# A four-layer attention and ReLU network on one core: reciprocals of two chunks spread by one set of DMAs, add and ReLU fused on VectorE, queues in a new order

## The chip, the cores and the metric

The kernel runs on one core of a Trainium2 chip. The metric is the time of one execution on the device, in microseconds (us); the median of several runs is compared. In the profile PE is TensorE (matmuls) and PEld its weight loads, DVE is VectorE, ACT is ScalarE, POOL is GpSimd, and SP is SyncE, which here only issues DMAs. "L960" is line 960 of the kernel before.

## What is computed

Four layers, each added to the residual x of 2048 tokens by 512: linear attention with 32 heads of 16, a feed-forward block with ReLU, and the same two again with the same weights.

```python
def _A_ref(x, wqkv, wo):
    qkv = (x @ wqkv).reshape(B, S, 3, H, Dh).transpose(2, 0, 3, 1, 4)   # H = 32, Dh = 16
    q, k, v = qkv[0], qkv[1], qkv[2]
    phi = lambda t: jnp.where(t > 0, t + 1, jnp.exp(t)) + 1e-6
    pq, pk = phi(q), phi(k)
    kv = jnp.einsum("bhsd,bhse->bhde", pk, v)
    z = jnp.einsum("bhsd->bhd", pk)
    num = jnp.einsum("bhqd,bhde->bhqe", pq, kv)
    den = jnp.einsum("bhqd,bhd->bhq", pq, z)[..., None] + 1e-6
    return (num / den).transpose(0, 2, 1, 3).reshape(B, S, D) @ wo

def _B_ref(x, w1, w2):                      # Dff = 1376
    return jnp.maximum(x @ w1, 0) @ w2

x = x + _A_ref(_layernorm(x), A_wqkv, A_wo)
x = x + _B_ref(_layernorm(x), B_w1, B_w2)
x = x + _A_ref(_layernorm(x), A_wqkv, A_wo)
x = x + _B_ref(_layernorm(x), B_w1, B_w2)
```

## The kernel before

**Tiling.** The 2048 tokens are 16 tiles of 128 (on the partitions), and four chunks of four tiles. The residual `xres` stays on chip in float32, the normalized input `xn` and its transpose `Tb` in float16. Layers 0 and 2 are attention, layers 1 and 3 the feed-forward block. Steps of a layer start as soon as the chunks that they need are there, so the end of one layer and the start of the next share the engines.

**Attention** goes in this order. For each chunk the keys and queries are projected (L980, L1193; some chunks by a seven-product scheme, L1032, whose last step on DVE is an `em` and a `phi`), and the sums over all tokens that give G are built up as chunks arrive (`g0_m_t`, `g1_m_t`, L1132; the 0 and 1 are the two halves of the keys, m a block of the input, t a chunk). In the steps `pq` and `bar` (L1758, L1780) the row of G for the normalization is evicted (`gevz`), gives z (`zcol`, `zc`), and with it the denominators: `den t` (L1216) multiplies the queries of chunk t by z on PE, with a block of 32 columns of the array per head group; ACT takes the logarithm (`lnd`, L1222) and the exponential of its negative (`rdc`, L1224), which is the reciprocal. One reciprocal belongs to 16 rows of the queries (the 16 positions of a head), and a tile of `rdc` has each of them four times; so a DMA spreads each block of 32 rows over 128 partitions (`spread t_j`, L1230, four DMAs of 128 KB per chunk, issued by SP). DVE multiplies the queries with the spread reciprocals, two blocks j at a time (`pqs t_0`, `pqs t_2`, L1237, line 1242 in the profile). Beside that PE combines G with the value weights (`kv`, L1158; for it DVE has subtracted a row from them in four parts, `wvless0` to `wvless3`, L1115), DVE masks the result (`kvmask0`, `kvmask1`, L1165), PE multiplies it by wo (`m0` to `m3`) and it is evicted as Mf (`mev`). Last, in the step `p2` (L1804), `fin i_0` and `fin i_2` (L1245) multiply the queries of tile i by Mf, four matmuls of 128x512 per tile (ps<-Mf,big in the profile, 64 of them), and `resid i` (L964) adds the residual. Then come the statistics of the next normalization (ACT squares, POOL and DVE the small ones, `rstd`, `nbias`), the normalization itself (`norm i`, L886), and the transposing DMA (`tr t_k`, L902) that the next layer's first matmul needs.

**The feed-forward block** computes x @ w1 in a seven-product scheme over 2x2 blocks (`b_h7`, L1396). Of its four quarters two leave PSUM by a plain ReLU (`hc11`, `hc21`, L1428) and two by an addition (`hc12`, `hc22`, L1437): a partial product in PSUM plus another that ACT saved in SBUF. The sum is written without ReLU, and when the second of the two is there, one more instruction applies ReLU to the whole row of both, in place (`hc22r`):

```python
def add(name, cs, bank, other, okeys, second, half, first):
    ...
    g.add(DVE, lambda e: e.tensor_tensor(ap, sh(psv[:, bank, 0:w]), sh(other()), ALU.add), ...
    if half == 0:
        first_half[0] = qk
        return
    ...
    g.add_flex([(ACT, lambda e: e.activation(row, row, ACTF.Relu), ...),
                (DVE, lambda e: e.tensor_scalar(row, row, 0.0, None, ALU.max), ...)], ...
```

The second product (`b_out`, L1563) has seven products per chunk too, after sums on DVE (`ssum`, L1530).

**What sets the order.** Each operation is entered in program order with the keys that it reads and writes, and gets a priority: its place in that order plus a hint from the table `HINTS` (L63, L445), by its name with the layer in front. Each engine's queue, SP's too, is sorted by priority, and each engine takes the first of its queue alone (`WINDOW` is 1 everywhere, L60), so an instruction that waits holds up all behind it on its engine. An operation with several engines to choose from (`add_flex`, L454) takes the one that a hint ending in "!" names. The durations in the file serve a planner (`_list_schedule`, L465) that gives out PSUM banks and fixes the waits.

Of the kernel before, what the change touches and what calls it, by code (L numbers as in the profile page):

```python
# [6 lines left out]

# [55 lines left out]
HINTS = {"0.aqsum1": -44, "0.aqsum1!": 0, "0.aqsum2": -5, "0.aqsum2!": 0, "0.aqsum3": -114, "0.aqsum3!": 0, "0.aqsum4": 0,  # L63
# [546 lines left out]
def build_kernel(nc, A_x, A_wqkv, A_wo, B_w1, B_w2, out, n_layers_pairs=2, K_STT=0, Q_STT=0, windows=None,  # L610
# [20 lines left out]
    with es:  # L631
# [11 lines left out]
        GT = sb("GT", [128, 4, 512], BF16)  # L643
        KVT = sb("KVT", [128, 4, 128], BF16)
        Mf = sb("Mf", [128, 4, 512], BF16)
        NL = 2
        FIN_SPLIT = 4
        SPLIT_H = 4
        SPLIT_TREV = 1
# [106 lines left out]
        def unit_ap(u, p=128):  # L756
            return big[0:p, u * 512:(u + 1) * 512]
# [638 lines left out]
        def b_h7(t, tw):  # L1396
# [40 lines left out]
            def add(name, cs, bank, other, okeys, second, half, first):  # L1437
# [3 lines left out]
                def sh(x):  # L1441
                    return x.rearrange("p (a k) -> p a k", k=256)
# [539 lines left out]
```

## Time and profile before

| | us |
|---|---|
| median of 3 runs | 261.85 (261.5 to 262.0) |
| profiled execution, first to last instruction (span) | 260.5 |
| PE busy | 255.2 (98%) |
| DVE busy | 230.8 (89%) |
| ACT busy | 206.3 (79%) |
| POOL busy | 60.0 (23%) |

The profiled execution's time is given as its span; what lies around the span is not recorded. Busy times are unions of the intervals in which an engine has an instruction in work. A matmul is drawn to the modelled end of its pipeline, so two that follow each other at full rate overlap. Some matmul records are missing (125 of 128 matmuls with Mf are there), which leaves short gaps that are none. In a row of the timeline "x16" says that 16 instructions of one kind are merged, and the bracket at its end how long the engine stood idle before it, and what ended that. A row of the table by stretches gives for each engine busy time and count, then the granted clock of PE, the share of the DMA engines and GB/s.

### The profile page before, as it was taken

How to read it: one execution, taken by the hardware profiler on the slowest of the kernel's cores; microseconds unless marked ns; L12 is line 12 of the kernel's file. 1: busy time of each engine (PE TensorE's matmuls, PEld its weight loads, DVE VectorE, ACT ScalarE, POOL GpSimd, SP SyncE). 2: the span in 40 equal slices, each digit the busy share in tenths (PEclk: the TensorE clock that was granted, in tenths of full speed). 3: DMA queues.
4: the chain of work that ended last, by engine and by line, in shares of the span. 5: the costliest groups of instructions: out<-in, count | busy, mean ns of one | idle time of the engine just before them, and what ended most of it. 6: DMA issues, size and time to landing. Idle time of an engine off the chain costs nothing.

```text
span 260.5 us, 5876 instructions
## 1 busy us (share of the span) xinstructions
PE 255.2 (98%) x2165; PEld 198.3 (76%) x2176; DVE 230.8 (89%) x572; ACT 206.3 (79%) x446; POOL 60.0 (23%) x163
## 2 busy tenths in 40 slices
PE   7999999999999999999999999999999999999995
PEld 3554577744788988889888878674388989888884
DVE  5999997799999999999989999858999998876684
ACT  4999999689999969999998899766899928853100
POOL 4100000037844015341420430003777000000000
PEclk9999999999999999999999999999999999999999
DMA  6767950754343062222130040057251414300104
GB/s 195 288 161 140 324 183 18 178 122 94 65 89 64 17 86 44 40 42 43 31 72 0 4 81 1 3 136 174 59 102 38 83 23 126 58 20 3 81 3 161
DMA packets 46268, 22.46 MB, mean 86 GB/s; under 512 B 35904, under 2 KB 44704, under 8 KB 46240
## 3 DMA queue, kind: packets, MB, share of 16 engines
q1 hardware_dynamic: 45968, 21.83, 34.8%
q10 hardware_dynamic: 272, 0.26, 0.4%
q8 instruction: 17, 0.28, 0.4%
q14 instruction: 11, 0.09, 0.1%
HBM read 7.14 MB, written 2.10 MB: 35 GB/s over the span
## 4 chain that ended last, share of the span: by engine, by line
PE 82%; DVE 5%; DMA 4%; SPq 4%; ACT 3%; issue 1%; DVEq 0%
PE ps L960 81%; SPq L1234 4%; DMA big<-rdc 3%; DVE xres L967 3%; DVE big L1242 1%; ACT lnd L1222 1%; DMA xin<-in_A_x_dram 1%; PE ps L919 1%; ACT rdc L1224 1%; DVE bst L851 0%; ACT big L1073 0%; DVE xin L1391 0%; PE ps L846 0%; ACT escr L1090 0%; ACT GT L1144 0%
## 5 line engine op out<-in xcount | busy, mean ns | idle before, releaser
L975 ACT ACTIVATE sqscr<-xres 128x512 bf16<-128x512 f32 x48 | 29.7, 621 | 4.4 <-DVE xres L967 3.0
L960 PE MATMUL ps<-w,big 128*128 128x256 bf16 (+1 forms) x256 | 32.6, 272 | 0.0
L960 PE MATMUL ps<-big,xn 128*128 128x256 bf16 (+1 forms) x221 | 31.6, 287 | 0.3
L702 ACT ACTIVATE ps<-ps 128x512 f32<-128x512 f32 (+1 forms) x41 | 22.7, 563 | 11.1 <-PE ps L960 11.1
L960 PE MATMUL ps<-Mf,big 128*128 128x512 bf16 x125 | 28.8, 379 | 0.7 <-DVE big L1242 0.5
L960 PEld LDWEIGHTS ps<-w,big 128*128 128x128 bf16 (+1 forms) x256 | 24.9, 98 | 3.1
L960 PEld LDWEIGHTS ps<-big,xn 128*128 128x128 f16 x224 | 21.5, 98 | 6.1 <-issue 0.7
L1443 DVE TENSOR_TENSOR big<-ps,escr 128x512 bf16<-128x512 f32 (+1 forms) x38 | 22.7, 600 | 3.6 <-PE ps L960 2.3
L960 PEld LDWEIGHTS ps<-Mf,big 128*128 128x128 bf16 x128 | 12.0, 98 | 15.8 <-DVE big L1242 2.0
L960 PE MATMUL ps<-Tb,w 128*128 128x256 f16 x160 | 23.7, 273 | 0.0
L960 PE MATMUL ps<-xn,xin 128*128 128x256 f16 x160 | 23.2, 273 | 0.0
L960 PE MATMUL ps<-xn,w 128*128 128x256 f16 x160 | 22.4, 273 | 0.0
L873 POOL TENSOR_SCALAR mean<-s 128x2 f32<-128x2 f32 x24 | 8.4, 350 | 56.0 <-DVE xres L967 53.5
L899 ACT ACTIVATE xn<-xres,nbias,rstd 128x512 f16<-128x512 f32 x26 | 20.7, 816 | 0.7 <-POOL nbias L883 0.6
L1462 ACT ACTIVATE escr<-ps 128x512 f32<-128x512 f32 (+1 forms) x38 | 19.2, 536 | 2.4 <-PE ps L960 2.3
L1431 ACT ACTIVATE big<-ps 128x512 bf16<-128x512 f32 (+1 forms) x38 | 19.0, 533 | 1.9 <-PE ps L960 1.8
L960 PE MATMUL ps<-wqkv,Tb 128*128 128x512 bf16 (+1 forms) x93 | 19.7, 342 | 0.1
L881 POOL TENSOR_TENSOR rstd<-veps,nhalf 128x2 f32<-128x2 f32 x24 | 18.4, 768 | 5.1 <-DVE veps L879 4.5
L960 PEld LDWEIGHTS ps<-Tb,w 128*128 128x128 bf16 x160 | 15.5, 98 | 2.5 <-DVE w L1391 0.4
L960 PE MATMUL ps<-w,Tb 128*128 128x96 bf16 (+2 forms) x176 | 17.3, 224 | 0.0
L960 PEld LDWEIGHTS ps<-xn,w 128*128 128x128 bf16 x160 | 15.4, 98 | 2.0
L960 PEld LDWEIGHTS ps<-xn,xin 128*128 128x128 bf16 x160 | 15.2, 98 | 2.0 <-DVE xres L967 0.2
(146 smaller groups left out, 626.1 us busy)
## 6 DMA issues: line engine op xcount, KB each, us to landing
big<-rdc SPq DMA_DIRECT2D x32, 128.0 KB, 2.7
w<-in_B_w_dram SPq DMA_DIRECT2D x1, 1376.0 KB, 7.2
w<-in_B_w_dram SPq DMA_DIRECT2D x1, 1280.0 KB, 10.4
xin<-in_A_x_dram SPq DMA_DIRECT2D x2, 512.0 KB, 6.5
wqkv<-in_A_wqkv_dram SPq DMA_DIRECT2D x3, 256.0 KB, 4.9
xin<-in_A_x_dram SPq DMA_DIRECT2D x4, 128.0 KB, 3.1
xin<-in_A_x_dram SPq DMA_DIRECT2D x2, 256.0 KB, 4.9
wqkv<-in_A_wqkv_dram SPq DMA_DIRECT2D x1, 512.0 KB, 4.1
```

Of the source, the lines that this page charges most:

```text
L702: g.add(ACT, lambda e: e.activation(psv[:, b, 0:w], psv[:, src, 0:w], ACTF.Identity), [("ps", src)], [("ps", b)], C_ACT_PSUM if w == 512 e ...
L873: g.add(POOL, lambda e: e.tensor_scalar(mean[:, sl], s1[:, sl], -INV_D, None, ALU.mult), [("s1", i) for i in tl], [("mean", i) for i in tl ...
L881: g.add(POOL, lambda e: e.tensor_tensor(rstd[:, sl], veps[:, sl], nhalf[:, 0:n], ALU.pow), [("veps", lo), ("nhalf",)], [("rstd", i) for i ...
L899: (ACT, lambda e: e.activation(xn[:, i, :], src, ACTF.Identity, scale=rstd[:, i:i + 1], bias=nbias[:, i:i + 1]), C_ACT_SB_AP)],
L919: last = e.transpose(psb()[:, 128 * q:128 * q + 128], xn[:, i, 128 * c:128 * c + 128], ident[:])
L960: last = e.matmul(o, l, r, start=st, stop=sp, skip_group_check=skip)
L967: g.add(DVE, lambda e: e.scalar_tensor_tensor(xres[:, i, :], psv[:, b, :], 0.0, src, ALU.add, ALU.add, accum_out=s1[:, i:i + 1]), [("ps", ...
L975: g.add(ACT, lambda e: e.activation(sqscr[:, q, :], xres[:, i, :], ACTF.Square, scale=math.sqrt(INV_D), accum_out=s2[:, i:i + 1]), xr(i), ...
L1234: dma(lambda e, j=j, u=u: e.dma_start(unit_ap(u), rdc[32 * j:32 * j + 32, t, :].unsqueeze(1).broadcast_to([32, 4, 512])), [("rdc", t)], [( ...
L1431: g.add_flex([(ACT, lambda e: e.activation(ap, src(), ACTF.Relu), C_ACT_PSUM if w == 512 else 270.0), (DVE, lambda e: e.tensor_scalar(ap, ...
L1443: g.add(DVE, lambda e: e.tensor_tensor(ap, sh(psv[:, bank, 0:w]), sh(other()), ALU.add), [("ps", bank)] + okeys + ([] if first else bk), q ...
L1462: g.add(ACT, lambda e, w=w: e.activation(q[:, 0:w], psv[:, bank, 0:w], ACTF.Identity), [("ps", bank)], key, C_ACT_PSUM if len(cs) == 2 els ...
```

## The change

Three parts, and a new table of hints.

*Spreads.* The reciprocals of chunks 0 and 1 are computed first, and each of the four DMAs then spreads both chunks, 256 KB instead of 128. The rows of both chunks lie side by side in source and target, so a DMA has as many descriptors as before, of twice the length. Chunk 2 and chunk 3 stay as they were.

```diff
+        SPREADS = ((0, 1), (2,))
...
-        def a_spread(t, first_layer):
-            late = 500.0 if first_layer and t == 0 else 0.0
+        def a_spread(t, n=1):
             for j in range(4):
                 u = rb_unit(t, j)
-                dma(lambda e, j=j, u=u: e.dma_start(unit_ap(u), rdc[32 * j:32 * j + 32, t, :].unsqueeze(1).broadcast_to([32, 4, 512])),
-                    [("rdc", t)], [("big", u)], 650.0, "spread%d_%d" % (t, j), issue=620.0, late=late)
+                dma(lambda e, j=j, u=u: e.dma_start(big[:, u * 512:(u + n) * 512],
+                                                    rdc[32 * j:32 * j + 32, t:t + n, :].rearrange("p n k -> p (n k)").unsqueeze(1)
+                                                    .broadcast_to([32, 4, 512 * n])),
+                    [("rdc", t + k) for k in range(n)], [("big", u + k) for k in range(n)], 650.0 * n, "spread%d_%d" % (t, j), issue=620.0)
...
-                        for u in range(NCH - 1):
-                            a_den(u)
-                            a_spread(u, first_layer)
+                        for grp in SPREADS:
+                            for u in grp:
+                                a_den(u)
+                            a_spread(grp[0], len(grp))
```

*Add and ReLU.* The additions `hc12` and `hc22` of layers 1 and 3 become one VectorE instruction that adds and clamps the sum to the range from 0 to the largest float32; the row ReLU `hc22r` goes.

```diff
+                if H_SAT:
+                    g.add(DVE, lambda e: e._custom_dve(dve_ops.TENSOR_ADD_SAT, out=ap, in0=sh(psv[:, bank, 0:w]), in1=sh(other()), s0=FMAX, s1=0.0),
+                          [("ps", bank)] + okeys + ([] if first else bk), qk + (bk if first else []),
+                          C_DVE_PSUM if len(cs) == 2 else 335.0, name="%s_%d_%d" % (name, t, cs[0]))
+                    return
```

*More choices.* The first normalization of tiles 6 to 15 and the four `wvless` may run on POOL; by the hints `fnorm8` and `fnorm9` do, `wvless` stays on DVE. Which engine computes the reciprocal root of the first normalization is written as a list, with the same result as before.

```diff
-                g.add_flex([(DVE, f, C_DVE_NORM_BF)],
+                g.add_flex([(DVE, f, C_DVE_NORM_BF)] + ([(POOL, f, C_POOL_NORM)] if i >= PE_TILES else []),
```

*Hints.* Of 1584 hints for places that both tables have, 59 are the same. Of the choices of an engine in layers 1 and 3, 13 of the plain ReLUs (`hc11`, `hc21`) move to DVE and 7 to ACT; the eviction `trev2` of the head, a copy of a transposed tile, moves to DVE. Some hints of layer 0, with the place that they give (place in program order plus hint; lower goes first):

| | before | after |
|---|---|---|
| den0, den1, den2 (PE) | 299, 321, 319 | 291, 298, 301 |
| spread2_2, spread2_3 (SP) | 331, 334 | 314, 310 |
| spread0_0 to spread0_3 (SP) | 324, 320, 314, 310 | 319, 323, 330, 326 |
| pqs2_2, wvless3, kvmask0 (DVE) | 358, 163, 326 | 332, 337, 346 |
| pqs3_0, pqs3_2, resid4, resid6 (DVE) | 432, 435, 416, 428 | 409, 415, 418, 428 |
| last of spread3, load of w2 (L805), tr0_0 (SP) | 407, 199, 434 | 389, 392, 422 |

Sorted by these, and by those of their neighbours, the queues stand as follows around the change (a group `g0_1_2` or `q7_3_4` is four matmuls of 128x256, g0_3_t four of 128x512).

```
layer 0, SP   before  spread0 (x4), spread2 (x4), spread1 (x4), spread3 (x4)      [w2 long before]
              after   spread2_3, spread2_2, spread0 with 1 (x4), spread2_1, spread2_0, spread3 (x4), w2, tr0_0, tr0_1
layer 0, PE   before  q7_2_4 g0_2_1 q7_3_7 den0 g0_0_3 g0_1_3 g0_2_2 g0_2_3 q7_3_4 kv0_0 kv0_1 kv0_2 den2 den1 kv0_3 g1_0_0
              after   q7_2_4 zcol g0_2_1 g0_2_2 den0 g0_1_2 g0_0_3 den1 den2 q7_3_7 g1_2_0 g0_2_3 g0_1_3 g1_0_0 g1_0_1 g1_2_1
                      g1_0_2 kv0_0 g1_0_3 kv0_1 q7_3_4 g1_1_0 kv0_2 g1_1_1 g1_1_2 kv0_3
              before  kv1_1 fin1_0 kv1_2 kv1_3 fin0_0 m2 m3 den3 fin2_0
              after   kv1_1 m1 m0 kv1_2 kv1_3 den3 m3 m2 fin0_0 fin2_0
layer 0, DVE  after   qc7_3_22_add wvless2 pqs2_2 wvless3 qc7_3_21_em qc7_3_21_phi kvmask0 kvmask1 pqs0_0 pqs1_0 pqs0_2 pqs1_2
layer 2, SP   before  spread0_0 0_1 1_1 1_0 0_3 0_2 1_2 1_3 2_3 2_2 2_0 2_1 3_1 3_3 3_2 3_0
              after   spread0 with 1 (x4) spread2_2 2_3 2_1 2_0 3_0 3_2 3_3 3_1
layer 2, PE   before  den0 den1 den2 ... m1 den3
              after   den0 den1 q7_3_7 kv0_0 kv0_1 g1_2_1 g1_0_1 g1_0_2 kv0_2 kv0_3 q7_3_4 g1_0_3 g1_1_0 g1_1_1 g1_1_2 g1_1_3 m0 den2
                      g1_2_2 g1_2_3 m1 kv1_0 kv1_1 den3
layer 2, DVE  before  resid1 resid0 pqs2_2 resid2 resid3 pqs2_0 resid4 resid5 nbias0 resid7 resid6 var4 pqs3_0 veps4 nbias2 pqs3_2
              after   resid1 pqs2_2 resid0 pqs2_0 resid3 var0 resid2 resid4 nbias0 pqs3_2 pqs3_0 resid5
head, PE      before  trp2 qh0_0_0_0 qh0_0_3_0 trp3         after  trp2 qh0_0_0_0 qh0_0_2_0 qh0_0_3_0 trp3 kproj2
```

More of the change, by code (lines that the diff above doesn't have):

```diff
@@ L6 @@
 from concourse import alu_op_type
+from concourse import dve_ops
 ALU = alu_op_type.AluOpType
@@ L646, in build_kernel @@
         NL = 2
+        SPREADS = ((0, 1), (2,))
+        H_SAT = True
+        FMAX = 3.4028234663852886e38
         FIN_SPLIT = 4
@@ L654, in build_kernel @@
         MID_LAST = ()
-        FIRST_ACT_TILES = 4
+        RSTD_ACT = (0, 1, 2, 3, 6, 8, 12)
+        PE_TILES = 6
         lnd = sb("lnd", [128, NL, 512], F32)
@@ L1116, in wv_less_last @@
             for m in range(4):
-                g.add(DVE, lambda e, m=m: e.tensor_tensor(wqkv[:, m, 2 * D:3 * D], wqkv[:, m, 2 * D:3 * D], wvl[:], ALU.subtract),
-                      [("wv0",), ("wvl",)], [("wv", m)], 335.0, name="wvless%d" % m)
+                f = (lambda e, m=m: e.tensor_tensor(wqkv[:, m, 2 * D:3 * D], wqkv[:, m, 2 * D:3 * D], wvl[:], ALU.subtract))
+                g.add_flex([(DVE, f, 335.0), (POOL, f, C_POOL_ADD)], [("wv0",), ("wvl",)], [("wv", m)], name="wvless%d" % m)
         def ones_col(lo, n):
@@ L1676, in ln_first @@
             for i in range(4 * t, 4 * t + 4):
-                if t < FIRST_PE_CHUNKS and i < 6:
+                if i < PE_TILES:
                     ln_stats_first(i, [("xn", i - 2)] if 2 <= i < 4 else [])
@@ L1684, in ln_first @@
             if t == 1:
-                ln_part_first(6, 8)
-                ln_norm(6, True)
-                ln_norm(7, True)
-                tr_dma(1, 1)
+                for i in range(PE_TILES, 8, 2):
+                    ln_part_first(i, i + 2)
+                    ln_norm(i, True)
+                    ln_norm(i + 1, True)
+                    tr_dma(1, i // 2 - 2)
             if t >= FIRST_PE_CHUNKS:
@@ L1815, in p2 @@
                         a_den(NCH - 1)
-                        a_spread(NCH - 1, first_layer)
+                        a_spread(NCH - 1)
                         a_pqs(2)
```

4 lines of the change are left out of this document (2 added, 2 removed), and 519 rows, old and new, of the table HINTS.

## The prediction

> **What bounds the kernel now.** I read the page first (part 1, part 4), then the table by stretches of 5 us, the waits, and the timeline of the two stretches that the table singles out. In order: two lines of the page; five stretches (PE busy, then PE's weight loads, DVE, ACT, POOL, granted clock, DMA share, GB/s); two rows of the waits.
>
> ```profile
> PE 255.2 (98%) x2165; PEld 198.3 (76%) x2176; DVE 230.8 (89%) x572; ACT 206.3 (79%) x446; POOL 60.0 (23%) x163
> ...
> PE 82%; DVE 5%; DMA 4%; SPq 4%; ACT 3%; issue 1%; DVEq 0%
> ...
> 60.00:65.00 5.00, 4.92 (x24) 2.07 (x23) 5.00 (x14) 4.93 (x15) 3.60 (x8) 1.00 0.46 88
> 80.00:85.00 5.00, 5.00 (x48) 4.46 (x46) 4.93 (x10) 5.00 (x11) 0.83 (x2) 1.00 0.30 57
> 180.00:185.00 5.00, 4.82 (x23) 1.98 (x21) 3.99 (x13) 2.92 (x10) 3.04 (x11) 1.00 0.42 100
> 185.00:190.00 5.00, 4.70 (x22) 1.98 (x21) 5.00 (x19) 5.00 (x14) 4.66 (x11) 1.00 0.54 103
> 195.00:200.00 5.00, 5.00 (x48) 4.49 (x47) 4.96 (x14) 5.00 (x14) 4.33 (x11) 1.00 0.34 67
> ...
> DVE big L1242 <- DMA big<-rdc: 3.7, 3, 1.9
> PEld ps L960 <- DVE big L1242: 2.0, 3, 0.8
> ```
>
> The reader is to see that PE is the bound: 98% busy, and 82% of the chain. In dense stretches (80:85, 195:200) it is busy 5.00 of 5.00 at granted clock 1.00, though DVE and ACT beside it are at 4.93 to 5.00 as well: their load costs nothing there. The change touches no matmul, so it can win only where PE stands still. The two gaps of the table, 180:185 and 185:190 (and a small one in 60:65), lie where attention's last product (ps<-Mf,big) waits for L1242, the product with the spread reciprocals, and L1242 waits for the spread DMAs. The timeline of layer 2 and, last, of layer 0:
>
> ```profile
> 169.98 11.41 SPq L1234 DMA_DIRECT2D big<-rdc  x16
> 176.44 6.21 PE L960 MATMUL ps<-Mf,big 128*128 128x512 bf16 x27
> 182.08 0.69 DVE L1242 TENSOR_TENSOR big<-big 128x1024 bf16<-128x1024 bf16 x1 [1.01 <-DMA big<-rdc]
> 182.83 3.14 PEld L960 LDWEIGHTS ps<-Mf,big 128*128 128x128 bf16 x16 [0.67 <-DVE big L1242]
> 182.83 3.63 PE L960 MATMUL ps<-Mf,big 128*128 128x512 bf16 x16 [0.18 <-DVE big L1242]
> 186.02 0.68 DVE L1242 TENSOR_TENSOR big<-big 128x1024 bf16<-128x1024 bf16 x1
> 186.76 3.13 PEld L960 LDWEIGHTS ps<-Mf,big 128*128 128x128 bf16 x16 [0.79 <-DVE big L1242]
> 186.76 3.63 PE L960 MATMUL ps<-Mf,big 128*128 128x512 bf16 x16 [0.30 <-DVE big L1242]
> ...
> 62.81 1.19 PEld L960 LDWEIGHTS ps<-Mf,big 128*128 128x128 bf16 x7 [0.57 <-DVE big L1242]
> ```
>
> One 128x512 matmul is drawn 0.38 long (its pipeline's end) but follows the last after (3.63 - 0.38) / 15 = 0.217 us. So the row from 176.44 ends its last start at 182.27, the next was due at 182.49 and came at 182.83: **a hole of 0.35**. The next row should have been followed at 182.83 + 16 x 0.217 = 186.30 and was at 186.76: **0.46**. Weight loads were idle 0.67 and 0.79 before these two, 0.32 more than the hole; the 0.57 before 62.81 therefore means **0.25** in layer 0. Together 1.06 us, all ended by L1242. That is what this change can reach; nearly all the rest of PE's time is matmuls.
>
> **The change part by part.** (1) *Spreads merged.* Per attention layer twelve issues for chunks 0 to 2 become eight; four carry two chunks.
>
> ```profile
> L1234 SPq DMA_DIRECT2D big<-rdc x32: 543/605/1203, 43.5 to 180.3; - x32
> DMA to landing us min/median/max: 2.6/2.7/4.6
> ...
> 177.46 4.60 DMA big<-rdc
> ...
> 170.48 0.63 ACT L1224 ACTIVATE rdc<-lnd 128x512 bf16<-128x512 f32 x1
> ...
> 170.00:178.00 8.00, 7.95 (x68) 5.37 (x67) 4.88 (x10) 5.19 (x10) 0.00 (x0) 1.00 0.72 161
> ...
> 43.51 13.22 SPq L1234 DMA_DIRECT2D big<-rdc  x15
> 46.85 0.69 DVE L1242 TENSOR_TENSOR big<-big 128x1024 bf16<-128x1024 bf16 x1 [0.83 <-DMA big<-rdc]
> ```
>
> An issue takes 0.605 on SP and, with the gap to the next, 0.65. In layer 2 the twelve filled SP from 169.98 to 178.04, and the last of them, issued at 177.46, landed 4.60 later, at 182.06: L1242 at 182.08 had waited for just that one. After: the merged four start when chunk 1's reciprocal is done (170.48 + 0.63 = 171.1 in the old order; den0 now has two groups of four matmuls fewer before it, 0.43 each, so about 170.4). Chunk 2's den now stands ten such groups behind, at about 173.0; an eviction and two activations of 0.6 put its reciprocal at 175.0: issued to 177.5, the last landed at 176.9 + 2.7 = 179.6, its product done by 180.4. When is it due? Without the holes the last product of this stage ends at 186.76 + 16 x 0.217 - 0.81 = 189.4. Chunk 2 has 40 matmuls left when it begins: due at 189.4 - 40 x 0.217 = 180.7. Chunk 3, with 20 left, is due at 185.1; its spreads start near 177.9 and land by 182.6. So both holes of layer 2 close: **-0.35 and -0.46**. In layer 0 chunk 3's products move ahead of two residual adds that stood before them: **-0.25**.
>
> What a merged transfer takes no row shows: no more than a single one (0.65, SP's pace), or twice (1.3). I take 1.0, between them and nearer to twice, since the DMA engines were at 0.72 in 170:178. In layer 2 the last merged one then lands at 170.4 + 2.7 + 3 x 1.0 = 176.1 and its product is done at 176.8; due at 177.2 (56 matmuls left). It is late from 1.15 up (C).
>
> (2) *Den matmuls regrouped.* They use 32 columns of the array, and the weight loads pause around each group.
>
> ```profile
> 41.77 0.10 PEld L960 LDWEIGHTS ps<-big,Zc 128*32 128x32 bf16 x4 [0.21 <-issue]
> 42.10 1.64 PEld L960 LDWEIGHTS ps<-big,xn 128*128 128x128 f16 x16 [0.23 <-issue]
> 44.73 0.61 PE L960 MATMUL ps<-big,Zc 128*32 128x512 bf16 x8
> 168.25 0.83 PE L960 MATMUL ps<-big,Zc 128*32 128x512 bf16 x12
> ```
>
> The loads stand idle 0.21 before den0 and 0.23 after it. Half of each is the lead that a load has over its matmul and loses here; the rest, 0.1, is PE's: 0.2 per group. Layer 0 keeps three groups (0; 1 and 2; 3). Layer 2 goes from two (0, 1 and 2 in one row of twelve; 3) to three: **+0.2**.
>
> (3) *Add and ReLU in one.* 48 adds of the last-stage quarters (hc12, hc22) become the fused instruction, and 24 row ReLUs go (10 on ACT, 14 on DVE). The add, an instruction with two stages and the same shapes, and the two wide ReLUs:
>
> ```profile
> L1443 DVE TENSOR_TENSOR big<-ps,escr 128x512 bf16<-128x512 f32 x26 | 17.7, 684 | 1.9 <-PE ps L960 1.6
> L967 DVE SCALAR_TENSOR_TENSOR xres<-ps,xres 128x512 f32<-128x512 f32 x16 | 10.3, 686 | 0.1
> L1452 ACT ACTIVATE big<-big 128x1024 bf16<-128x1024 bf16 x7 | 7.4, 1059 | 0.9 <-DVE big L1443 0.9
> L1453 DVE TENSOR_SCALAR big<-big 128x1024 bf16<-128x1024 bf16 x9 | 3.8, 417 | 0.0
> ```
>
> The fused form is not in the trace. Below: the plain add, 684; the two-stage instruction takes 686; above: add plus half a row's ReLU, 684 + 417 / 2 = 893. I take 686, the nearest in kind. DVE then loses 9 x 417 + 5 smaller ones, about 5 us, ACT 7 x 1059 + 3 smaller, about 9 us; by their hints about 3 us of other ReLUs move from ACT to DVE. Worth **0**: PE had no hole beside them (195:200). What hides DVE's work is that PSUM's banks let PE run on. At 893 DVE would pay at most 8 us more, 6 net; it stands idle 260.5 - 230.8 = 29.7 over the span, so PE would lose 0 to about 1, which the high end takes in.
>
> (4) *Queues reordered.* Almost every hint differs, so almost every queue does; PE's work stays, and I price the places where a new wait stands in line. Layer 0: DVE's product of chunk 2 (pqs2_2) goes ahead of wvless3, chunk 3's last phi and kvmask0, and waits for two spreads that SP now issues first. den0 stood at 41.77 and loses two groups before it: 40.9; den2 follows at 42.6. Four activations of 0.6 put rdc2 at 44.4, the second spread starts at 45.05 and lands at 47.7, its product and wvless3 are done at 48.8; the matmul that needs it (kv0_3), thirteen groups and three small ones behind den2, is due at 49.0. Nothing, but with 0.2 of cover. Layer 0's kvmask1 and the head:
>
> ```profile
> 52.19 0.11 PEld L960 LDWEIGHTS ps<-wo,KVT 128*128 128x128 bf16 x2 [0.58 <-DVE KVT L1166]
> 9.20 0.23 PEld L919 LDWEIGHTS ps<-ident,xn 128*128 128x128 f16 x4 [0.26 <-DVE xn L889]
> ```
>
> 0.58 idle, a hole of 0.25 behind kvmask1, filled in part by fin0_0; after, den3 stands in its place and is as long: 0. In the head one transpose waited 0.26 of the loads' time for its normalization; a further product stands before it, but the copy behind it moves to DVE and is late by as much: 0 (gain at most 0.15). GpSimd takes two normalizations of chunk 2 from DVE; the projections that need them stand behind those of the other two tiles, 1.7 us of matmuls: 0. In three places (wvless3 and den2 of layer 0, chunk 2's products in layer 2) work and need tie within 0.3, worth 0 to 0.3 each: I add **+0.2** for the three.
>
> Sum: -0.35 - 0.46 - 0.25 + 0.2 + 0.2 = **-0.7 us**. The profiled execution spans 260.5; the median of the timed runs is 261.85, so 1.35 lie around the span and stay. 261.85 - 0.7 = **261.15**. A difference of under 0.2% (0.5 us) is about what a measurement of this kernel can't tell from no change.
>
> **Rivals.**
> *A. DVE blocked in layer 0.* If the second spread takes not 2.7 but up to the longest, 4.6, wvless3 ends at up to 50.7 and PE stands up to 1.7. I take 1.3: 262.45. It decides from a landing of 2.9. For it: 46.85 shows DVE waiting 0.83 for a spread in this very place; against: the longest belonged to the twelfth of a burst, these are the first.
>
> *B. w2's load before the transposes; the slower end.* In layer 0 the load L805 moves from 26 us to right behind chunk 3's spreads, ahead of tr0_0 and tr0_1.
>
> ```profile
> w<-in_B_w_dram SPq DMA_DIRECT2D x1, 1280.0 KB, 10.4
> ...
> Tb<-xn SPq DMA_TRANSPOSE x29, 3.1
> ...
> 25.00:37.00 12.00, 11.89 (x77) 7.45 (x77) 12.00 (x33) 12.00 (x25) 0.12 (x1) 1.00 0.90 293
> 61.52 2.65 SPq L904 DMA_TRANSPOSE Tb<-xn  x2
> 66.31 1.05 PE L960 MATMUL ps<-Tb,w 128*128 128x256 f16 x8
> ```
>
> At the 293 GB/s of the old place 1.31 MB need 4.5 us: issued at about 57 (rdc3 near 54.4, then four spreads), it is through by 63.5, and tr0_0, issued at 61.52, lands at its median 3.1 later, 64.6. If it takes its 10.4 (w1 stood before it then), to 67.4, tr0_0 lands near 68.4, and layer 1's first matmul, due at 66.31 - 0.25, waits 2.3: 261.15 + 2.3 = 263.4. It decides from w2 landing at about 65.
>
> *C. Merged means late.* Chunk 0's spreads now wait for chunk 1's reciprocal: their first issue goes from 43.51 to about 45.6 in layer 0. At 1.3 per transfer layer 2's second product is done at 177.7, 0.5 late; with the longest landing, 1.9 more, 2.4. I take 1.4: 262.5. The Trainium skill ("Perfetto Trace Analysis", section "DMA Optimizations") says that splitting a DMA lets some parts start sooner where the engines are mostly idle, which speaks against merging. The trace agrees in part: L1242 did start on chunk 0 alone, at 46.85, but the engines were at 0.72 in 170:178, not idle, and no run yet shows the merged form.
>
> *D. Nothing moves.* The holes close and others of their size open, since these orders are tight everywhere: 261.85.
>
> *E. All holes close*, the small ones of the head and of kvmask1 too: 261.15 - 0.15 - 0.25 - 0.2 = 260.5.
>
> **How the numbers follow.** Forecast 0.59 (260.6 to 261.7), E 0.04, D 0.10, A 0.11, B 0.08, C 0.08. Faster: E and the forecast below 261.33, 0.04 + 0.53 = 0.57. Same: the rest of the forecast and D, 0.16. Slower: A, B and C, 0.27. Low end 259.9: E with the scatter of the runs before (261.5 to 262.0). High end 262.9: A and C are in it, B is left out.
>
> **What would show it.** Right: PE at 5.00 in the stretches that answer to 180:190, and no L1242 in the weight loads' waits; fused adds near 686; eight issues where there were twelve. Step 1 is wrong if L1242 still waits for big<-rdc with PE behind it; step 3 if the fused rows are above 750 and DVE shows ahead of PE in layers 1 or 3; step 4 if PE shows idle time before kv0_3, or before layer 1's first matmul with Tb<-xn as its releaser. A PE total other than about 255 us would upset the whole argument.

## The result, and the profile after

| | before | after |
|---|---|---|
| median (14 runs each, same chip), us | 262.07 | 263.16 (262.66 to 265.32) |
| ratio of the means, 95% interval | | **1.0058** (1.0040 to 1.0075) |
| span of the profiled execution, us | 260.5 | 261.4 |
| PE busy, us | 255.2 | 255.7 |
| layer 1's first matmul, us | 66.31 | 67.10 |
| from there to the end of layer 2's attention, us | 124.1 | 124.1 |

The kernel became slower, by 0.4% in the medians and 0.6% in the means: the forecast was 261.15. The last two rows say where. All of the profiled execution's 0.8 us is lost before layer 1 begins, about half of it before 35 us, where two executions of one kernel differ by more than that (before_again below). In layer 2 the holes of the prediction went, and others of about their size came. From the end of layer 2's attention to PE's last matmul both traces take 67.49.

The page of after (part 1, the shares of the chain), the waits, the transfers, and the stretches (PE, its loads, DVE, ACT, POOL, granted clock, DMA share, GB/s):

```profile
PE 255.7 (98%) x2166; PEld 199.0 (76%) x2176; DVE 229.7 (88%) x570; ACT 197.0 (75%) x429; POOL 65.1 (25%) x158
...
PE 89%; DMA 5%; ACT 2%; DVE 1%; SPq 1%; issue 0%; ACTq 0%
```

```profile
DVE big L1163 <- DMA big<-rdc: 2.2, 5, 1.2
PEld ps L880 <- DVE big L1163: 2.3, 5, 0.7
```

```profile
big<-rdc SPq DMA_DIRECT2D x16, 128.0 KB, 2.9
big<-rdc SPq DMA_DIRECT2D x8, 256.0 KB, 4.6
```

```profile
50.00:55.00 5.00, 4.64 (x33) 2.16 (x32) 4.36 (x9) 4.04 (x8) 0.00 (x0) 1.00 0.66 191
60.00:65.00 5.00, 4.95 (x24) 2.29 (x24) 5.00 (x15) 4.62 (x11) 3.89 (x10) 1.00 0.85 253
175.00:180.00 5.00, 4.50 (x30) 1.96 (x29) 4.01 (x8) 3.23 (x6) 0.00 (x0) 1.00 0.79 216
180.00:185.00 5.00, 4.95 (x24) 2.29 (x24) 4.77 (x16) 3.75 (x10) 2.65 (x7) 1.00 0.51 108
185.00:190.00 5.00, 5.00 (x25) 2.29 (x24) 4.93 (x16) 4.98 (x14) 4.42 (x14) 1.00 0.44 80
```

What the reader is to see: 180:185 and 60:65 are full but for 0.05 and 185:190 wholly, as forecast, and the product L1163 (L1242 before) is still what PE's weight loads wait for. The loss moved to 175:180 (0.50) and 50:55 (0.36). A merged transfer takes a median of 4.6 us to land, a single one 2.9. The timeline of after at the two new places, DVE and PE (the bracket of a PE row counts from a modelled end, so a hole is the bracket and 0.38 - 0.217 = 0.16 more):

```profile
53.82 1.29 DVE L1163 TENSOR_TENSOR big<-big 128x1024 bf16<-128x1024 bf16 x2 [0.26 <-DMA big<-rdc]
175.92 0.69 DVE L1163 TENSOR_TENSOR big<-big 128x1024 bf16<-128x1024 bf16 x1 [0.29 <-DMA big<-rdc]
176.67 0.60 PE L880 MATMUL ps<-Mf,big 128*128 128x512 bf16 x2 [0.50 <-DVE big L1163]
```

The four merged transfers of layer 2 landed at 174.28, 175.90, 176.56 and 177.77: the first 3.67 after its issue at 170.61, and (177.77 - 174.28) / 3 = 1.16 apart. The *first* product needs the second of them, 175.90; before, the two single ones that it needs were there at 173.27. The first output projection starts at 176.67, 0.50 + 0.16 after PE was free: **0.67** by the unrounded times. The chain of waits says the same for both layers:

```profile
47.50 1.26 SPq L1153
48.81 4.99 DMA big<-rdc
53.82 0.70 DVE big L1163
...
171.22 4.67 DMA big<-rdc
175.92 0.70 DVE big L1163
```

### The profile page after: what moved, and what is told of

It reads as the page before. It is cut to its first block, busy times and chain, and to the rows that moved or that the text cites. A ratio compares the mean times of both kernels' runs of the same rounds, so it can differ in the third digit from the quotient of the medians.

```text
span 261.4 us, 5833 instructions
## 1 busy us (share of the span) xinstructions
PE 255.7 (98%) x2166; PEld 199.0 (76%) x2176; DVE 229.7 (88%) x570; ACT 197.0 (75%) x429; POOL 65.1 (25%) x158
## 4 chain that ended last, share of the span: by engine, by line
PE 89%; DMA 5%; ACT 2%; DVE 1%; SPq 1%; issue 0%; ACTq 0%
PE ps L880 88%; DMA big<-rdc 4%; SPq L1153 1%; ACT rdc L1144 1%; DMA xin<-in_A_x_dram 1%; ACT lnd L1142 1%; PE ps L839 1%; DVE big L1163 1%; DVE bst L771 0%; PE ps L766 0%; ACT big L993 0%; DVE rdc L1543 0%; DVE mv L772 0%; DVE xn L809 0%; ACT GT L1074 0%
## 5 line engine op out<-in xcount | busy, mean ns | idle before, releaser
L1365 DVE CUSTOM_DVE_ANT_0 big<-ps,escr 128x512 bf16<-128x512 f32 (+1 forms) x38 | 22.8, 602 | 2.9 <-PE ps L880 1.7
L1352 ACT ACTIVATE big<-ps 128x512 bf16<-128x512 f32 (+1 forms) x32 | 16.9, 532 | 10.3 <-PE ps L880 6.7
L880 PE MATMUL ps<-xn,w 128*128 128x256 f16 x160 | 23.3, 272 | 0.0
L819 ACT ACTIVATE xn<-xres,nbias,rstd 128x512 f16<-128x512 f32 x27 | 21.5, 813 | 2.2 <-POOL nbias L803 1.7
L793 POOL TENSOR_SCALAR mean<-s 128x2 f32<-128x2 f32 x24 | 7.1, 299 | 49.5 <-DVE xres L887 48.3
```

Of the source, the lines that this page charges most:

```text
L793: g.add(POOL, lambda e: e.tensor_scalar(mean[:, sl], s1[:, sl], -INV_D, None, ALU.mult), [("s1", i) for i in tl], [("mean", i) for i in tl ...
L819: (ACT, lambda e: e.activation(xn[:, i, :], src, ACTF.Identity, scale=rstd[:, i:i + 1], bias=nbias[:, i:i + 1]), C_ACT_SB_AP)],
L880: last = e.matmul(o, l, r, start=st, stop=sp, skip_group_check=skip)
L1352: g.add_flex([(ACT, lambda e: e.activation(ap, src(), ACTF.Relu), C_ACT_PSUM if w == 512 else 270.0), (DVE, lambda e: e.tensor_scalar(ap, ...
L1365: g.add(DVE, lambda e: e._custom_dve(dve_ops.TENSOR_ADD_SAT, out=ap, in0=sh(psv[:, bank, 0:w]), in1=sh(other()), s0=FMAX, s1=0.0), [("ps", ...
```

## The experiments

The theory when they began (theory 1 in the texts below): the merged transfers' late landing is what costs, as in rival C of the prediction. Its rivals: the new order of the queues costs by itself, or the fused instruction does, by a fixed time around the span (theory 2). Kernels sent together share a chip and the runs of before; ratios are to before, of the means, with their 95% interval.

### The parts one by one: b_fused, a_unmerged, a_addonly, b_merged2

b_fused is before with the fused instruction alone. a_unmerged is after with each chunk spread by itself, chunk 1's four spreads right behind chunk 0's. a_addonly is after with the plain add in the fused one's place; it leaves the ReLU of these quarters out. b_merged2 is before with chunks 0 and 1 merged in layer 2 alone.

```diff
 a_unmerged
-                        for grp in SPREADS:
+                        for grp in ((0,), (1,), (2,)):
 a_addonly
-  g.add(DVE, lambda e: e._custom_dve(dve_ops.TENSOR_ADD_SAT, out=ap, in0=sh(psv[:, bank, 0:w]), in1=sh(other()), s0=FMAX, s1=0.0),
+  g.add(DVE, lambda e: e.tensor_tensor(ap, sh(psv[:, bank, 0:w]), sh(other()), ALU.add),
 b_merged2
-                        for u in range(NCH - 1):
+                        for grp in ((0,), (1,), (2,)) if first_layer else ((0, 1), (2,)):
```

> The kernel before with the fused add and ReLU alone: the 24 ReLU instructions of the second inner quarters leave ScalarE and VectorE, all queues otherwise in before's order. Theory 2 (the new kind of instruction costs a fixed time around the span): the time around the span rises from 1.35 to 1.74 us, 262.45 against 262.07, the span unchanged within 0.1. Rival (the time around the span has another cause, or is different from run to run): 262.0 to 262.1 with 1.35 around the span.

> The changed kernel with the merging alone undone: chunk 0's four transfers of 128 KB stand where the merged ones stood, chunk 1's four right behind them; every queue's order is otherwise that of the changed kernel. Theory 1 (the merged transfers land too late for the first products): pqs0_0 of layer 2 no longer waits for its transfer, the PE holes at 175.95 (0.67 us) and 54.11 (0.25 us) shrink by about 0.3 and 0.25, and the time is 262.6 against 263.16 of the changed kernel; the holes of the kernel before at the products of chunks 2 and 3 (0.35, 0.46 and 0.25 us) may come back in part, up to 263.4. Rival (the loss lies in the order of the queues or in the fused instruction): the two holes stay and the time is 263.1 or more without any L1153 transfer showing up.

> The changed kernel with each fused add and ReLU replaced by a plain add of the same operands at the same place; the ReLU of the second inner quarters is left out. Theory 2: the time around the span falls from 1.74 to 1.35 us and the time to 262.75. Rival: unchanged, 263.1 to 263.2, with 1.74 around the span. In either case the mean of these 38 instructions stays near 600 ns and the PE holes stay where they are.

> The kernel before with layer 2's spreads of chunks 0 and 1 merged in pairs (four transfers of 256 KB for eight of 128 KB, at the places where chunk 0's stood), nothing else. Theory 1: the first issue waits for rdc1 (171.1 instead of 170.0), the two transfers that the first product reads land at about 174.8 and 176.4 instead of 172.56 and 173.27, the product runs at 176.4 instead of 173.29 and the first output projection starts 1.8 us late; against it the holes at 182.27 and 186.08 (0.35 and 0.46 us) close: 263.0 against 262.07 of before. My forecast's step 1 (merged transfers cost nothing ahead of the first product and close the two holes): 261.3.

| | median, us (runs) | ratio |
|---|---|---|
| b_fused | 262.02 (12) | 1.0004 (0.9985 to 1.0023) |
| a_unmerged | 262.91 (12) | 1.0037 (1.0022 to 1.0052) |
| a_addonly | 263.46 (7) | 1.0054 (1.0030 to 1.0079) |
| b_merged2 | 266.35 (5) | 1.0164 (1.0136 to 1.0192) |

**The fused instruction is free.** b_fused equals before, a_addonly stays where after is, and in the lines of after and of before the largest group of fused instructions is as long as that of the adds. Nor does it add a fixed time: the profiled execution takes 1.74 us more than its span in b_fused and in a_addonly alike. The lines:

```profile
L1365 DVE CUSTOM_DVE_ANT_0 big<-ps,escr 128x512 bf16<-128x512 f32 (+1 forms) x38 | 22.8, 602 | 2.9 <-PE ps L880 1.7
```

```profile
L1443 DVE TENSOR_TENSOR big<-ps,escr 128x512 bf16<-128x512 f32 (+1 forms) x38 | 22.7, 600 | 3.6 <-PE ps L960 2.3 <-ACT escr L1462 1.0
```

**The order costs.** a_unmerged and b_fused both have the fused form and single transfers; little but the hints differs (the order, and which engine takes an operation), and the means are 0.33% apart: 0.9 us. The traces place it: layer 1 starts at 67.05 in a_unmerged and 66.59 in b_fused (0.46, though a_unmerged lost 0.2 less in the first 12 us), and from there to the end of layer 2's attention it takes 123.61 against 123.26 (0.35).

**Merging put into the old order costs most**, far more than expected. Timeline of b_merged2, DVE and PE, and its stretches:

```profile
177.00 0.69 DVE L1244 TENSOR_TENSOR big<-big 128x1024 bf16<-128x1024 bf16 x1 [5.04 <-DMA big<-rdc]
178.08 0.47 PE L960 MATMUL ps<-GT,wqkv 128*128 128x128 bf16 x4 [2.44 <-DVE GT L1155]
```

```profile
175.00:178.00 3.00, 0.64 (x8) 0.24 (x8) 1.00 (x3) 0.60 (x1) 0.00 (x0) 1.00 0.86 216
178.00:182.00 4.00, 3.92 (x14) 1.60 (x15) 2.98 (x6) 0.85 (x2) 0.00 (x0) 0.57 0.55 147
```

In this order DVE stands 5.04 us at the first product, and the evictions of g1, which the next matmuls with GT need, stand behind it: PE is idle for 2.44, in 175:178. Then its granted clock is 0.57 of full speed in 178:182, and 512-column matmuls start 0.427 apart, twice 0.217, for some 3.5 us: 1.7 us more. The expectation had neither the queue behind the product nor the clock. The Trainium skill ("TensorE: Matmul & The Clock Gate", section "Part 1: The HAM clock gate (the "warmup" mystery)") has the clock fall to a half after an idle window of about 3.4 us; here 2.44 us without a matmul was enough.

### Does it repeat, and can the order be mended: before_again, after_again, a_local, b_best

a_local is a_unmerged with hints that put back what looked costly: in layer 0 the eviction `gevz` on ScalarE, chunk 0's spreads ahead of chunk 2's, DVE's products in the order in which PE needs them, and `kvmask1` ahead of a sum of weights (`2.aksum2`); in layer 2 `gev1_0` on ScalarE. b_best is b_fused with layer 1's sum of weights `1.usum1` later on DVE.

```diff
 a_local, hints
-"0.gevz!": 1, "0.spread2_2": 7, "0.spread2_3": 2, "0.pqs0_0": -7, "0.pqs0_2": 1, "0.pqs2_2": -82, "2.aksum2": -371, "2.gev1_0!": 1
+"0.gevz!": 0, "0.spread2_2": 24.875, "0.spread2_3": 23.25, "0.pqs0_0": -33.5, "0.pqs0_2": -20, "0.pqs2_2": -52, "2.aksum2": -366.5, "2.gev1_0!": 0
 b_best, hints
-"1.usum1": -28
+"1.usum1": -10.5
```

> The kernel before once more, for a second profiled execution. My forecast's step 1 (the PE holes at 182.27 and 186.08 belong to the kernel and recur): both stand again, 0.35 and 0.46 us, with a VectorE product waiting about 1.0 us for a spread. Rival (one spread landed 1.7 us later than usual in that one execution): the two holes are missing, as in the profile of the kernel before with the fused instruction, and the span is about 0.5 us shorter, near 260.0. Time 261.9 to 262.1 in either case.

> The changed kernel once more, on the chip of the other three, for a second profiled execution. Theory 1 (merged transfers and queue order): 263.1 to 263.2; the hole ahead of layer 2's first output projection is 0.6 to 0.7 us again, with the product behind the merged transfer; the one near 54.1 in layer 0 stands again (0.25, or up to the 0.75 of the plain-add run). Rival (single late transfers): one of the two is gone.

> The changed kernel with the merging undone and five places of its queues set back towards the kernel before: the evacuation ahead of zcol in layer 0 on ScalarE, not VectorE; chunk 0's spreads ahead of chunk 2's in layer 0, and its products ahead of chunk 2's; kvmask1 ahead of 2.aksum2; the evacuation gev1_0 of layer 2 on ScalarE. Theory (the reordering costs about 0.9 us, the difference between the run with the merging undone, 262.91, and the run of before with the fused instruction, 262.02, and these five places hold most of it): zcol's hole (0.15 us) and layer 2's last one (0.29 us) close, the one after den3 falls from 0.39 to 0.25, together 262.2. Rival (the order costs elsewhere, in the head or in small pieces): 262.7 to 262.9.

> The kernel before with the fused add and ReLU, and layer 1's first weight sum (0.74 us on VectorE) moved behind the last products of layer 0. Reading of the traces: the hole at 62.3 (0.25 us in the trace of before, 0.36 with the fused instruction) comes from VectorE being late, not from a transfer, since the transfers of chunk 3 had landed 1 us ahead of their product: the hole closes, 261.7 against 262.0. Rival (my forecast: the product waits for its transfer there): the hole stays, 262.0.

| | median, us (runs) | ratio |
|---|---|---|
| before_again | 261.99 (12) | 1.0006 (0.9984 to 1.0027) |
| after_again | 263.62 (6) | 1.0064 (1.0043 to 1.0085) |
| a_local | 262.37 (12) | 1.0018 (0.9998 to 1.0038) |
| b_best | 262.45 (12) | 1.0025 (1.0004 to 1.0045) |

The result repeats. What does not repeat is layer 2 of before. The chain of b_best has the late transfer of the prediction again, and its product and PE's hole; the timeline of before_again, with before's own queues, runs through:

```profile
177.60 4.43 DMA big<-rdc
```

```profile
182.06 0.69 DVE L1243 TENSOR_TENSOR big<-big 128x1024 bf16<-128x1024 bf16 x1 [0.84 <-DMA big<-rdc]
```

```profile
178.87 13.14 PE L960 MATMUL ps<-Mf,big 128*128 128x512 bf16 x60
```

Sixty of these matmuls follow without a gap in before_again, 13.14 - 0.38 = 59 x 0.216. So **the 0.81 us that the forecast meant to gain in layer 2 are there in one execution and not in the next**: of five traces with layer 2's old queues, before and b_best show them (0.64 in b_best), and before_again, b_fused and b_norm3 (below) don't. Layer 1's first matmul to the end of layer 2's attention takes 124.08 in before and 123.27 in before_again.

No run moved that landing, but the traces show what stands beside it. In each burst of spreads, in all sixteen traces, one packet of 16 KB of the kind "instruction" goes over a queue of its own (q8) and takes 0.9 to 1.6 us, and no 128-KB spread lands between 0.9 and 2.0 us after that packet's start. In before it starts at 180.05, when the twelfth transfer, issued at 177.46, was just due; that one lands at 182.06. In before_again it starts at 181.68; the twelfth still lands 0.85 later, after its usual 2.6, and the thirteenth is held up. The packet in the DMA view of before, 180.0:180.1 (count, MB, and its time as a share of 16 engines over 0.1 us, which makes 0.96 us):

```profile
q8 instruction: 1, 0.02, 60.1%
```

Time alone does not tell which transfer is held up: the packet comes 0.7 us before the twelfth is due in b_best, where it is late, and 0.8 before in b_fused, where it is not. That the packet is the cause is likely and not shown.

The start of the kernel differs too. Before_again's profiled execution took 263.88, the longest of its twelve, and its layer 1 starts at 68.73, 2.4 us later than in before with the same queues. PE's first transpose came at 5.65 instead of 5.05, since DVE waited 0.49 for the input, and the first eight matmuls of 512 columns went at half the pace, although the granted clock reads 1.00 there. Timelines of before and of before_again:

```profile
6.33 1.93 PE L960 MATMUL ps<-wqkv,Tb 128*128 128x512 bf16 x8
```

```profile
7.33 3.47 PE L960 MATMUL ps<-wqkv,Tb 128*128 128x512 bf16 x8
```

PE's gaps, summed from start to start less 0.217 us per 512 columns, come to 1.5 between 4.4 and 12 us in before and to 3.6 in before_again, to 1.7 in after and after_again. So the start of layer 1 compares two kernels only once this is taken off.

Against such an execution without the late landing, after loses in layer 2 as well: 124.06 - 123.27 = 0.8. From 12 us to layer 1's first matmul the same gaps come to 1.8 in after and 2.0 in after_again, against 1.25 in before and 1.6 in before_again: 0.2 to 0.8 more. Together that makes 1.0 to 1.6, and the means are 0.58%, 1.5 us, apart.

b_best was to close the hole of layer 0 at 62 and come to 261.7. It closed it, but layer 1's first matmul then waited for the moved sum, a hole of 0.61 at 66.5. a_local wins back layer 0 (layer 1's first matmul at 66.14) and loses 0.57 in layer 2, where the wait moved from DVE to ScalarE, in its timeline of the loads:

```profile
175.61 0.11 PEld L880 LDWEIGHTS ps<-Mf,big 128*128 128x128 bf16 x2 [0.58 <-ACT Mf L1093]
```

### Merging and order taken apart by layer: a_um2, a_um0, a_l0

a_um2 is after with single transfers in layer 2 alone, a_um0 in layer 0 alone. a_l0 is a_local without its layer 2 edit: single transfers in both layers, layer 0's order mended, layer 2's as in after.

```diff
 a_um2, a_um0
-                        for grp in SPREADS:
+                        for grp in (((0,), (1,), (2,)) if layer in (2,) else SPREADS):        [0 for a_um0]
 a_l0, hints, against a_local
-"2.gev1_0": -14.5, "2.gev1_0!": 0
+"2.gev1_0": -14, "2.gev1_0!": 1
```

> The changed kernel with the merging undone in layer 2 alone. Theory: the merging's whole cost lies in layer 2, where the hole ahead of the first output projection falls from 0.7 to 0.29 us; in layer 0 it is neutral, since the product that waited for a merged transfer (0.26 us) waits for a single one instead when it is undone (0.59 us): 262.8 to 262.9, as with the merging undone in both layers. Rival (layer 0's merging costs as much): 263.0 to 263.2.

> The changed kernel with the merging undone in layer 0 alone. Reading of four traces with layer 0 merged: chunk 0's second product waits for the fourth merged transfer and the PE hole after it is 0.25, 0.45, 0.75 and 1.48 us, with the landing between 53.8 and 55.0. Theory (layer 0's merging costs too, by landings that scatter): no such hole near 54, at most 0.46 near 61 where a product waits for a single transfer; layer 2 keeps its hole of 0.7: 262.9 to 263.1, about 0.4 under the changed kernel on this chip. Rival (neutral in layer 0): 263.2 to 263.6, as the changed kernel.

> The changed kernel with the merging undone in both layers and layer 0's four places set back (zcol's evacuation on ScalarE; chunk 0's spreads and its products ahead of chunk 2's; kvmask1 ahead of 2.aksum2); layer 2's queues are those of the changed kernel. Theory (the reordering's cost sits in layer 0 where chunk 2's spreads go first and in layer 2's last evacuation): layer 0 ends near 66.3, layer 2's hole is 0.29 us, and the time is 262.0 to 262.2, within 0.2 of the kernel before. Rival (the rest of the order costs as much): 262.4 or more.

| | median, us (runs) | ratio | hole before layer 2's first output projection | layer 1's first matmul |
|---|---|---|---|---|
| after | 263.16 (14) | 1.0058 (1.0040 to 1.0075) | 0.67 | 67.10 |
| a_um2 | 263.38 (9) | 1.0055 (1.0030 to 1.0080) | 0.29 | 67.87 |
| a_um0 | 263.40 (12) | 1.0059 (1.0036 to 1.0081) | 0.69 | 67.70 |
| a_unmerged | 262.91 (12) | 1.0037 (1.0022 to 1.0052) | 0.29 | 67.05 |
| a_l0 | 262.20 (12) | 1.0010 (0.9988 to 1.0032) | 0.29 | 66.15 |

a_um2 and a_um0 came out some 0.4 us above what was expected. The last column has the start of the kernel in it: PE lost 1.7, 1.3, 2.0, 1.4 and 1.3 us there, between 4.4 and 12 us, in these five.

In **layer 2** the merge costs 0.4 us in the traces wherever it is (0.67, 0.73 and 0.67 in after_again and a_addonly too), and what is left without it, 0.29, is the order. The first product and the load behind it, timelines of a_unmerged:

```profile
175.50 0.68 DVE L1163 TENSOR_TENSOR big<-big 128x1024 bf16<-128x1024 bf16 x1
176.24 0.11 PEld L880 LDWEIGHTS ps<-Mf,big 128*128 128x128 bf16 x2 [0.29 <-DVE big L1163]
```

The product no longer waits for a transfer, it is just late in its queue.

In **layer 0** the theory that the merge costs fell. Merged, the hole at 54 us scatters from trace to trace: 0.25, 0.45, 0.75 and, in a_um2, 1.48, where one transfer took 6.24 us; single, in a_unmerged, DVE waits 0.59 for one of chunk 1's transfers, and the work that stands behind it on DVE leaves PE a hole of 0.46 at 61.8. Both transfers land 2.2 to 2.4 us after the instruction packet of their burst (52.20 and 52.23). Timelines of a_um2 and a_unmerged:

```profile
54.59 1.29 DVE L1163 TENSOR_TENSOR big<-big 128x1024 bf16<-128x1024 bf16 x2 [1.49 <-DMA big<-rdc]
55.34 1.47 PE L880 MATMUL ps<-Mf,big 128*128 128x512 bf16 x6 [1.31 <-DVE big L1163]
```

```profile
54.47 0.69 DVE L1163 TENSOR_TENSOR big<-big 128x1024 bf16<-128x1024 bf16 x1 [0.59 <-DMA big<-rdc]
```

What layer 0 loses is its **order**. With its four places put back, a_l0 starts layer 1 at 66.15, 0.9 before a_unmerged (0.7 of it after 35 us) and level with b_fused but for the start of the kernel, and over the whole run it is not told apart from before. (Its interval and a_unmerged's overlap by 0.1%; the traces carry this reading.) Loads of after (40.45 is of `zcol`) and of a_l0:

```profile
40.45 0.17 PEld L880 LDWEIGHTS ps<-ident,GT 128*128 128x128 bf16 x4 [0.27 <-DVE GT L1065]
52.42 0.11 PEld L880 LDWEIGHTS ps<-wo,KVT 128*128 128x128 bf16 x2 [0.51 <-DVE KVT L1086]
53.02 0.33 PEld L880 LDWEIGHTS ps<-Mf,big 128*128 128x128 bf16 x3 [0.48 <-DVE big L1163]
```

```profile
51.89 0.11 PEld L880 LDWEIGHTS ps<-wo,KVT 128*128 128x128 bf16 x2 [0.48 <-DVE KVT L1086]
```

In after PE waits for `gevz` on a full DVE (hole 0.16), and at 53.02 for chunk 0's product, since chunk 0's spreads start at 46.2 instead of 43.5, behind two of chunk 2's (hole 0.15). In a_l0 only the wait for KVT is left, which before has as well. Stretches of a_l0:

```profile
50.00:55.00 5.00, 4.81 (x34) 2.29 (x32) 4.82 (x12) 3.71 (x9) 0.00 (x0) 1.00 0.42 100
175.00:180.00 5.00, 4.88 (x26) 2.08 (x24) 4.34 (x11) 2.99 (x7) 0.00 (x0) 1.00 0.71 167
180.00:185.00 5.00, 5.00 (x25) 2.25 (x23) 4.86 (x16) 4.43 (x11) 3.88 (x9) 1.00 0.33 80
```

### A merge once more, in a mended order: a_best, a_best_m2

a_best is a_local with layer 2's `mev1` ahead of `lnd2` on ScalarE and `fin0_0` ahead of `m3` on PE. a_best_m2 is a_best with layer 2 merged again: the pair isolates the merge on one chip.

```diff
 a_best, hints
-"2.mev1": -3, "2.fin0_0": -9
+"2.mev1": -12.75, "2.fin0_0": -12
 a_best_m2
+                        for grp in (SPREADS if layer == 2 else ((0,), (1,), (2,))):
```

> The kernel with the merging undone and five places set back, and two more places of layer 2: the evacuation mev1 ahead of lnd2 on ScalarE, and the first half of fin0 ahead of m3 on TensorE. In its parent's trace the first output projection of layer 2 waited 0.58 us for mev1, behind gev1_0, lnd2 and rdc2. Theory (that wait only moved from VectorE to ScalarE): the hole falls from 0.57 to 0.1 and the time from 262.37 to 261.9, at or just under the kernel before (261.98). Rival (rdc2 half a microsecond later makes chunk 2's spreads late): a hole of 0.3 or more with L1163 as releaser between 178 and 182, 262.3.

> The same kernel with the merging put back in layer 2 alone (four transfers of 256 KB for eight of 128 KB), nothing else changed. Theory 1 (merged means late): the first issue waits for rdc1, 0.6 us later; the two transfers that the first product reads land 2.4 us later than the two small ones; the product waits for the second and the first output projection starts 0.4 to 0.7 us late: 0.4 to 0.6 above the same kernel without it. Rival (my forecast: cover is enough, and fewer issues help chunks 2 and 3): equal or up to 0.3 faster.

a_best: 263.27 (7), 1.0061 (1.0039 to 1.0082), where 261.9 was expected. `mev1` pushed chunk 2's reciprocal and so its spreads back, and PE lost 1.10 + 0.16 = 1.26 us at 182. a_best_m2: 264.00 (6), 1.0096 (1.0063 to 1.0129), 0.73 over a_best; the two intervals overlap. The loads before the first output projection of each, timelines:

```profile
175.28 0.55 PEld L880 LDWEIGHTS ps<-Mf,big 128*128 128x128 bf16 x4 [0.19 <-DVE big L1163]
182.44 1.90 PE L880 MATMUL ps<-Mf,big 128*128 128x512 bf16 x8 [1.10 <-DVE big L1163]
```

```profile
175.30 0.69 DVE L1163 TENSOR_TENSOR big<-big 128x1024 bf16<-128x1024 bf16 x1 [0.46 <-DMA big<-rdc]
176.04 0.55 PEld L880 LDWEIGHTS ps<-Mf,big 128*128 128x128 bf16 x4 [0.74 <-DVE big L1163]
```

The hole is 0.18 single and 0.74 merged, from a product that waits for its transfer again: 0.56 us is the price of the merge here, a little more than the 0.4 of the other traces.

### Before's hole in layer 0: b_norm3

The prediction put 0.25 us of layer 0 down to the spreads. The timeline of before has chunk 3's spreads landed by 60.05 and both products in one row without a wait, the second beside a GpSimd normalization. b_norm3 is b_fused with that normalization (norm3) on ScalarE.

```diff
-            if i % 4 == 3:
+            if i % 4 == 3 and not (g.layer == 0 and i == 3):
```

> The kernel before with the fused add and ReLU, and the second normalization of tile 3 in layer 0 on ScalarE (ahead of two of its sums of squares), not on GpSimd. Reading of four traces: layer 0's hole at 62.3 follows chunk 3's second product on VectorE, which takes 1.09 to 1.18 us there and 0.69 elsewhere, while GpSimd's normalization (1.27 to 1.32 us) runs beside it. Theory (the two engines hold each other up, no transfer is late): both products take 0.69, the hole of 0.25 to 0.36 closes, 261.7 against 262.0 of the kernel before on this chip. Rival (my forecast: a transfer is waited for there): the product stays at 1.1 or starts later, and the hole stays, 262.0.

```profile
60.95 1.27 POOL L894 TENSOR_SCALAR xn<-xres,mean,rstd 128x512 f16<-128x512 f32 x1
61.02 1.73 DVE L1242 TENSOR_TENSOR big<-big 128x1024 bf16<-128x1024 bf16 x2
```

```profile
62.15 1.29 DVE L1243 TENSOR_TENSOR big<-big 128x1024 bf16<-128x1024 bf16 x2
```

262.39 (12), 1.0011 (0.9992 to 1.0030). The two products take 1.29 in place of 1.73, and the hole is gone: it was DVE slowed beside GpSimd, not a transfer. Another of 0.46 opened at 69.8, where PE waits for a copy on ScalarE that now stands behind the moved normalization, so nothing was won.

## Why the prediction was wrong

*Bound.* Right: PE is at 98% before and after, and every loss found is PE standing still. Wrong in one point: it took one execution's holes for the kernel's. 0.81 of the 1.06 us hang on one landing that comes late in some executions, and 0.25 were no wait for a transfer (b_norm3).

*Step 1, the spreads merged, -1.06: the step that failed.* The holes went from 180:190 as worked out, since chunk 2's spreads came in time. But a merged transfer takes 1.16 (layer 2) to 1.27 us (layer 0: landings 49.99 to 53.80), not 1.0, with the "late from 1.15 up" of the prediction just behind; the first lands 3.67 after its issue, where 2.7 was taken; and the check was made for the last transfer and the second product, while the first product, due earlier, waits for the second transfer. Rival C (262.5, a chance of 0.08) has the mechanism of layer 2, merged means late, at another place: the second product, which it priced, waited 0.25 on DVE and cost PE nothing, and the first product's hole is 0.67, of which 0.4 is the merge. The rule of the Trainium skill ("Perfetto Trace Analysis", section "DMA Optimizations") that was cited with it, that a split transfer may let parts start sooner, holds here: the first single transfers were landed at 173.27, the first two merged at 175.90.

*Step 2, den regrouped, +0.2.* Agrees: layer 2 has three groups instead of two, and PE shows 0.1 ahead of each and 0.1 behind. Too small for a ratio of its own.

*Step 3, the fused instruction, 0.* Right: 602 ns against 600, b_fused 1.0004, a_addonly as after.

*Step 4, the queues, +0.2: mis-sized.* a_unmerged against b_fused gives about 0.9: 0.5 to 0.6 in layer 0, where a_l0 gets back all of it, and 0.35 in layer 2. The price list had looked at wvless3 and kv0_3 and let kvmask1 and the head pass; the costly places were `gevz` on DVE (0.15), and chunk 0's spreads behind two of chunk 2's, which made the *first* product of the stage late (0.15) and, in a_unmerged, a later one of chunk 1 (0.46); the need had been looked up for chunk 2 only.

*Around the span.* Not 1.35 but 1.7 to 1.8 in every run, before's too (262.15 with a span of 260.4): the span 260.5 belongs to about 262.25, not to the median 261.85. That moved the forecast by 0.4, though not its sign.

*Rivals.* A: DVE did stand 1.22 at chunk 2's product (48.19, landing 2.6), but PE was full in 45:50; nothing. B: the load of w2 took from 57.1 to 63.5, tr0_0 landed at 65.1; nothing, as the working there had it. D, that holes close and others of their size open, is what layer 2 did against before's own trace (124.1 in both); layer 0 lost beside it. E: no.

No version beat before. a_l0, with the merge undone and four places of layer 0's queues put back, is not told apart from it. Open: whether layer 0's merge costs on average (undoing one layer's merge alone shows nothing in the medians, undoing both gives 0.2%, and the intervals overlap), and whether the instruction packet is what makes single landings scatter.

## What to carry to other kernels

A transfer of twice the size in place of two saves issues, but its first half is ready only with its second: check the *first* consumer's due time against the later landing, not the last one's. Before you price a hole as a gain, look at a second trace of the same kernel, for a hole that a scattered landing makes is not the kernel's; and before you compare when a layer starts, take off what the start of the kernel lost in each trace. And where many queues are reordered at once, go through each engine for whose *first* need moved back; four places among some fifteen hundred changed hints held about 0.7 of the 0.9 us that the order cost.

## What the hardware showed beside that

- The granted clock fell after PE had stood still for only 2.44 us, and 512-column matmuls took twice as long for 3.5 (b_merged2).
- SP's issue of a spread takes 0.60 us as a rule. The fourth merged one of layer 2 took 1.58 to 1.63 in every trace that has it, and single ones reach 1.20 (before) to 1.83 (a_addonly).
- Two DVE products of 128x1024 in bf16 in a row take 1.29 us, and 1.73 beside one GpSimd normalization of 128x512 (b_norm3, before).
- The same transfer from the same place in the queue lands after 2.6 or after 4.6 us, a merged one after 3.7 to 6.2; in before the late one falls on a 16-KB packet of the instruction queue.
- Two executions of one kernel differ by 2.1 us in their first 12 us (before, before_again).
